# Idle transposes on TensorE in the first attention stage, with the first loads reordered

## The chip, the cores and the metric

The kernel runs on one core of one Trainium2 chip. A core has five engines that run their own instruction streams side by side [...]: TensorE (PE in the profile: matrix products, and transposes done as products with an identity), VectorE (DVE), ScalarE (ACT), GpSimd (POOL) and SyncE (SP, which here only issues DMA transfers). The metric is the device time of one execution in microseconds (us). Times of a kernel are given as the median of several executions, with the lowest and the highest. The profile is of one further execution, taken by the hardware profiler.

## The reference

The reference is attention with a threshold, followed by two dense layers with an ELU between them, all in float32:

```python
batch, n_heads, seq, head_dim = (8, 8, 576, 64)
scale = 1.0 / np.sqrt(q.shape[-1])
scores = scale * np.matmul(q, k.transpose(0, 1, 3, 2))
thresh = np.max(scores, axis=-1, keepdims=True) - tau
scores = np.where(scores >= thresh, scores, -1000000000.0)
scores = scores - np.max(scores, axis=-1, keepdims=True)
attn = np.exp(scores)
attn = attn / (np.sum(attn, axis=-1, keepdims=True) + 1e-09)
attn_out = np.matmul(attn, v)
# (B,H,S,D) -> (B*S, H*D): 4608 tokens of 512
h = x @ w_in                       # 512 x 2048
g = np.where(h > 0.0, h, alpha * (np.exp(np.minimum(h, 0.0)) - 1.0))
out = g @ w_out                    # 2048 x 512
```

`tau` is one number. The inputs of the dense layers' weights come as 64-bit floats and are converted to 32 bits on the chip, piece by piece.

## The kernel before

The kernel goes through 32 pairs of heads (8 sequences of 4 pairs). A pair has five steps: four with 128 queries of each of the two heads, and one with the last 64 queries of both. It is written in stages. The first stage is the first sequence, pairs 0 to 3, with only attention and some weight conversion in it; from the second stage on the dense layers' products are mixed in. In the first stage each head of a step passes through these parts, in the order that the framework's scheduler chooses (it orders by dependencies and its own estimates; the later stages stand under `manual_schedule`, where the order is the written one).

The start of the kernel: `tau` is read first and five small values are made of it, then the first pair's queries and keys are loaded and turned by VectorE, which puts the head dimension on the partitions:

```python
ident = wstage.tile([P, P], FP32, name="ident", bufs=1)
make_identity(nc, ident)

tau_sb = const.tile([P, 1], FP32, name="tau_sb")
nc.sync.dma_start(tau_sb, tau.to_broadcast([P, 1]))
pos = const.tile([P, 1], FP32, name="pos")
nc.vector.tensor_scalar(pos, tau_sb, 0.0, None, ALU.is_ge)
# ... keep, nkeep, far, ntau: five more small VectorE operations

def load(pr, parts=("qm", "km", "v"), shared=False):
    # ...
    for name, src in (("qm", q), ("km", k)):
        # ...
        for i in range(2):
            for d in range(2):
                r = (2 * i + d) * T
                nc.sync.dma_start(m[r : r + T],
                    src[b, 2 * j + i].rearrange("(j t) d -> t j d", t=T)[:, :, d * T : (d + 1) * T])
    # ... then four transfers of v into vm and vd

def prep_q(pr):   # VectorE turns the queries
    nc.vector.transpose(qT, raws[pr]["qm"].rearrange("p j d -> p (j d)"))
def prep_k(pr):   # and the keys
    nc.vector.transpose(kT[:, TAIL:], raws[pr]["km"].rearrange("p j d -> p (j d)"))

load(0)
prep(0)       # prep_q, copy_q, prep_k, copy_k
load(1)
```

The parts of one head in the first stage: scores on TensorE, maximum on VectorE, bias and bound on GpSimd, exponential on ScalarE, mask and sum on VectorE, division on GpSimd:

```python
def scores(pr, i, hs):
    # one of three PSUM buffers "sc"; two products of 288 keys for each head
    nc.tensor.matmul(scs[h][:, a, :HALF], qs[r], kT[r, k0 : k0 + HALF], start=True, stop=True)

def exponentials(pr, i, hs):
    nc.vector.tensor_reduce(st["mx"][:, cs], src[:, :, :, :HALF], axis=AX.XY, op=ALU.max)
    nc.gpsimd.tensor_scalar(st["nb"][:, cs], st["mx"][:, cs], nkeep, 1.0, ALU.mult, ALU.mult)
    nc.gpsimd.tensor_scalar(st["th"][:, cs], st["mx"][:, cs], 1.0, ntau, ALU.mult, ALU.add)
    nc.scalar.activation(e, st[h][:, :, :HALF], AF.Exp, bias=st["nb"][:, h : h + 1], scale=keep)

def masks(pr, i, hs):
    nc.vector.scalar_tensor_tensor(wv, sc[:, :, :HALF], st["th"][:, h : h + 1], e, ALU.is_ge, ALU.mult,
                                   accum_out=sm[:, h : h + 1])
    # ... 1 / (sum + 1e-9) into rs

def normalize(pr, i, hs):
    nc.gpsimd.tensor_scalar(wv, wv, st["rs"][:, h : h + 1], 1.0, ALU.mult, ALU.mult)
```

Then the weights `w` of a step are transposed on TensorE in groups of one to four 128x128 blocks. Each group has a PSUM buffer `rt` (two of them), and ScalarE copies it out to `wT`. A step of 128 queries has three groups (9 transposes), the step of the last queries has two (6):

```python
def transpose(dst, src):
    nc.tensor.matmul(dst, src, ident, is_transpose=True, skip_group_check=True)

def turn_parts(pr, i):
    # ...
    def room():
        return psum["t"].tile([P, NC, P], FP32, name="rt", tag="rt")

    def chunks(c0, c1):
        rt = room()
        for c in range(c0, c1):
            transpose(rt[:, c - c0], w[:, c * P : (c + 1) * P])
        return lambda: to(slice(g0, g0 + NT), slice(c0, c1), rt[:, : c1 - c0])   # ScalarE copies
    # ...
```

Last come the products with the values, `pv`, from `wT` (18 products for each half of a pair). The loop of the first stage:

```python
heads = [(pr, i, [h]) for pr, i in steps[:per_seq] for h in heads_of(i)]    # 36 heads
begin(*heads[0])                    # scores and exponentials
for n, (pr, i, hs) in enumerate(heads):
    if n + 1 < len(heads):
        begin(*heads[n + 1])
    # ... a piece of the dense layers' weights is loaded or converted now and then
    finish(pr, i, hs)               # masks and normalize
    if len(turned) > 1:
        behind(*turned.popleft())   # products with the values
    if n and hs == [0]:
        turn(*heads[n - 1][:2])     # transposes of the step before
        turned.append(heads[n - 1][:2])
```

## Time and profile before

| what | value |
|---|---|
| device time, median of 3 executions | 1376.99 us |
| lowest and highest | 1374.53 and 1379.93 us |
| span of the profiled execution | 1385.3 us |
| PE busy | 1338.2 us (97% of the span) |
| DVE busy | 1059.7 us (76%) |
| POOL busy | 834.4 us (60%) |
| ACT busy | 625.1 us (45%) |

Busy shares are averages over the whole span. The change touches the first stage alone, which in this profile takes about the first 112 us, so stretches of that part are what to read: the profile can give each engine's busy time for any stretch, and the timeline of an engine with the operation that it waited for. In such rows `sc` is the scores' product, `rt` a transpose, `pv` a product with the values; `x8` counts records, and a float32 matrix product of the scores or values leaves two records, a transpose one. Lines such as L238 are lines of the kernel's source. PEclk is the share of TensorE's full clock that was granted; it is shown as 1.00 where the trace holds no record of it, which is the case for the first 27.6 us.

### The profile page before, as it was taken

To read this page: it belongs to the slowest core of one execution; us is meant where nothing else is said; L and a number is where in the kernel's file an instruction comes from. 1 tells how busy PE (TensorE), PEld (TensorE's weight loads), DVE (VectorE), ACT (ScalarE), POOL (GpSimd) and SP (SyncE) were. 2 spreads that over 40 slices of the span, in tenths; PEclk is the share of its full clock that TensorE was granted. 3 is DMA by queue.
4 is the path that set the end of the run, shared out by engine and by line. 5 is a ranking of instruction groups with operands and counts; after the bars stand their busy time and mean duration, and the time that the engine had idled before them with its cause. 6 is when DMAs were issued, how large, how long until landed. Compare 5 with 4: busy or idle time off the path is not lost.

```text
span 1385.3 us, 21952 instructions
## 1 busy us (share of the span) xinstructions
PE 1338.2 (97%) x6566; PEld 993.5 (72%) x6566; DVE 1059.7 (76%) x2364; ACT 625.1 (45%) x1371; POOL 834.4 (60%) x1345
## 2 busy tenths in 40 slices
PE   7897889999999999999999999999999999999998
PEld 4554645746777777767777777777777777888886
DVE  6778885888879887869789878988888875545433
ACT  4666655225454554536363636354544453312320
POOL 4657774778657574747476756656575746425523
PEclk9999999999999999999999999999999999999999
DMA  5235552589798989898889989888889885321311
GB/s 114 58 72 143 142 143 62 165 239 263 221 253 222 273 221 241 225 256 235 225 234 249 251 225 256 225 239 216 250 234 263 232 243 172 123 69 55 102 57 31
DMA packets 316342, 259.82 MB, mean 188 GB/s; under 512 B 208320, under 2 KB 272320, under 8 KB 316224
## 3 DMA queue, kind: packets, MB, share of 16 engines
q1 hardware_dynamic: 316224, 258.42, 67.8%
q8 instruction: 53, 0.87, 0.3%
q14 instruction: 65, 0.53, 0.1%
HBM read 167.84 MB, written 90.51 MB: 186 GB/s over the span
## 4 chain that ended last, share of the span: by engine, by line
PE 79%; DVE 7%; POOL 4%; DMA 3%; ACT 3%; issue 2%; SPq 1%; DVEq 0%; POOLq 0%; ACTq 0%
PE f L1001 27%; PE f L846 25%; PE sc L238 12%; PE pv L388 8%; PE pv L384 2%; PE f L435 2%; PE f L475 2%; DMA there<-x 2%; DVE w L265 2%; PE rt L277 1%; ACT e L253 1%; POOL wtop L143 1%; POOL w L274 1%; DVE wtop L137 1%; DVE mx L248 1%
## 5 line engine op out<-in xcount | busy, mean ns | idle before, releaser
L274 POOL TENSOR_SCALAR w<-w,rs 128x576 f32<-128x576 f32 x288 | 246.1, 860 | 108.8 <-DVE rs L1111 75.2
L1085 DVE TENSOR_REDUCE mx<-sc 128x1 f32<-128x576 f32 x207 | 148.0, 752 | 88.5 <-PE sc L238 88.5
L238 PE MATMUL sc<-kT,qT 64*128 64x288 f32 x1024 | 185.5, 445 | 20.9 <-DVE w L265 11.5
L348 DVE STREAM_TRANSPOSE x<-w 128x512 f32<-128x512 f32 (+1 forms) x350 | 182.6, 569 | 8.2 <-POOL w L274 8.2
L1095 ACT ACTIVATE e<-sc,nb,keep 128x576 f32<-128x576 f32 x207 | 172.1, 831 | 7.0
L1104 DVE SCALAR_TENSOR_TENSOR w<-sc,th,e 128x576 f32<-128x576 f32 x207 | 163.4, 812 | 9.4 <-ACT e L1095 1.2
L1093 ACT ACTIVATE nb<-mx,nkeep 128x1 f32<-128x1 f32 x207 | 61.4, 297 | 233.0 <-DVE mx L1085 233.0
L238 PEld LDWEIGHTS sc<-kT,qT 64*128 64x128 f32 x1024 | 102.3, 193 | 86.5 <-issue 52.8
L846 PE MATMUL f<-xt,sw 128*128 128x256 f32 x512 | 128.8, 389 | 1.5 <-DMA sw<-win_sums 1.0
L846 PE MATMUL f<-xt,w_in_sb 128*128 128x256 f32 x512 | 124.5, 382 | 0.3 <-ACT w L860 0.2
L1089 POOL TENSOR_SCALAR th<-mx,ntau 128x1 f32<-128x1 f32 x207 | 54.4, 264 | 112.7 <-DVE mx L1085 112.5
L846 PEld LDWEIGHTS f<-xt,sw 128*128 128x128 f32 x512 | 93.3, 190 | 30.1 <-issue 14.6
L253 ACT ACTIVATE e<-sc,nb,keep 128x576 f32<-128x576 f32 x81 | 65.1, 830 | 104.7 <-POOL nb L249 103.9
L846 PEld LDWEIGHTS f<-xt,w_in_sb 128*128 128x128 f32 x512 | 96.1, 190 | 18.9 <-ACT xs L400 4.6
L1001 PE MATMUL f<-w_out_sb,s 128*128 128x256 f32 x448 | 109.4, 387 | 0.0
L1001 PE MATMUL f<-w_out_sb,g 128*128 128x256 f32 x448 | 107.4, 382 | 0.5 <-DVE g L901 0.5
L1001 PE MATMUL f<-t,s 128*128 128x256 f32 x448 | 106.6, 380 | 0.3 <-POOL s L938 0.3
L846 PE MATMUL f<-x,w_in_sb 128*128 128x256 f32 x448 | 105.8, 379 | 0.0
L1001 PEld LDWEIGHTS f<-w_out_sb,s 128*128 128x128 f32 x448 | 82.3, 190 | 23.0 <-issue 11.6
L1001 PEld LDWEIGHTS f<-w_out_sb,g 128*128 128x128 f32 x448 | 84.0, 190 | 16.6 <-issue 3.8
L865 POOL TENSOR_TENSOR u<-u,w 128x256 f32<-128x256 f32 x64 | 49.0, 766 | 77.3 <-ACT u L860 77.3
L1001 PEld LDWEIGHTS f<-t,s 128*128 128x128 f32 x448 | 84.1, 190 | 13.7 <-POOL s L938 2.7
(162 smaller groups left out, 2581.3 us busy)
## 6 DMA issues: line engine op xcount, KB each, us to landing
there<-x SPq DMA_DIRECT2D x500, 144.0 KB, 4.3
wTb<-there SPq DMA_DIRECT2D x75, 576.0 KB, 4.8
wTa<-there SPq DMA_DIRECT2D x50, 576.0 KB, 4.5
sw<-win_sums SPq DMA_DIRECT2D x62, 384.0 KB, 4.8
t<-wout_sums SPq DMA_DIRECT2D x45, 512.0 KB, 5.5
qm<-in_q_dram SPq DMA_DIRECT2D x128, 72.0 KB, 4.4
vm<-in_v_dram SPq DMA_DIRECT2D x64, 128.0 KB, 4.3
wst<-in_moe_w_in_dram SPq DMA_DIRECT2D x16, 512.0 KB, 4.6
```

The lines of the kernel that those rows point to most:

```text
L238: nc.tensor.matmul(scs[h][:, a, :HALF], qs[r], kT[r, k0 : k0 + HALF], start=True, stop=True)
L253: nc.scalar.activation(e, st[h][:, :, :HALF], AF.Exp, bias=st["nb"][:, h : h + 1], scale=keep)
L274: nc.gpsimd.tensor_scalar(wv, wv, st["rs"][:, h : h + 1], 1.0, ALU.mult, ALU.mult)
L348: nc.vector.transpose(x[:, :, c0 : c0 + nc_], src.rearrange("p (c g n) -> p g c n", c=nc_, n=T))
L388: nc.tensor.matmul(pv[h * D : (h + 1) * D, g0 * T : g1 * T], vm[:, h, c], wT[:, g0:g1, h * (NC + 1) + c], start=False, stop=(c == NC - 1), ...
L846: nc.tensor.matmul(loc["banks"][place], left[:, j], right[:, j], start=(begins and j == 0), stop=(j == 1), skip_group_check=True)
L1001: nc.tensor.matmul(place(m), lhs, rhs, start=(begins and v == 0), stop=(v == RU - 1), skip_group_check=True)
L1085: nc.vector.tensor_reduce(st["mx"][:, h : h + 1], st[h][:, :, :HALF], axis=AX.XY, op=ALU.max)
L1089: nc.gpsimd.tensor_scalar(st["th"][:, h : h + 1], st["mx"][:, h : h + 1], 1.0, ntau, ALU.mult, ALU.add)
L1093: nc.scalar.mul(st["nb"][:, h : h + 1], st["mx"][:, h : h + 1], nkeep)
L1095: nc.scalar.activation(e, st[h][:, :, :HALF], AF.Exp, bias=st["nb"][:, h : h + 1], scale=keep)
L1104: nc.vector.scalar_tensor_tensor(wv, sc[:, :, :HALF], st["th"][:, h : h + 1], e, ALU.is_ge, ALU.mult, accum_out=st["sm"][:, h : h + 1])
```

## The change

Three things change, all in the first stage.

1. Ahead of the first data, 28 transposes of the identity into an `rt` buffer are put on TensorE. Their results are never read. Each later group of transposes in the first stage gets four of the same ahead of it, into its own buffer, where the real ones then overwrite them. They are meant to keep TensorE active, and so its clock up, while it would otherwise wait.
2. The first pair's keys are loaded by ScalarE's DMA queue, beside the queries on SyncE's.
3. `tau` is read, and its small values made, after the first queries and keys have been asked for and turned; the values `v` of the first pair come after it. This opening now stands under `manual_schedule`.

```diff
-    tau_sb = const.tile([P, 1], FP32, name="tau_sb")
-    nc.sync.dma_start(tau_sb, tau.to_broadcast([P, 1]))
-    pos = const.tile([P, 1], FP32, name="pos")
-    nc.vector.tensor_scalar(pos, tau_sb, 0.0, None, ALU.is_ge)
     ... (the other small values)
+    def read_tau():
+        nc.sync.dma_start(tau_sb, tau.to_broadcast([P, 1]))
+        nc.vector.tensor_scalar(pos, tau_sb, 0.0, None, ALU.is_ge)
     ... (the other small values)
-    def load(pr, parts=("qm", "km", "v"), shared=False):
+    def load(pr, parts=("qm", "km", "v"), shared=False, queue=nc.sync):
     ...
-                    nc.sync.dma_start(
+                    queue.dma_start(
     ...
+    def idle(rt, n):
+        for _ in range(n):
+            transpose(rt[:, 0], ident)
+        return rt
     ...
         def room():
-            return psum["t"].tile([P, NC, P], FP32, name="rt", tag="rt")
+            return idle(psum["t"].tile([P, NC, P], FP32, name="rt", tag="rt"), 4 if "f" not in psum else 0)
     ...
-    load(0)
-    prep(0)
-    load(1)
+    with tc.manual_schedule():
+        load(0, ("qm",))
+        load(0, ("km",), queue=nc.scalar)
+        idle(psum["t"].tile([P, NC, P], FP32, name="rt", tag="rt"), 28)
+        prep_q(0)
+        prep_k(0)
+        copy_k(0)
+        copy_q(0)
+        read_tau()
+        load(0, ("v",))
+        load(1)
```

`"f" not in psum` holds in the first stage only. There are 54 groups of transposes in it, so 216 idle transposes beside the first 28.

## Prediction

> **What bounds the kernel now.** The page's chain that ended last is 79% PE, so I looked for where PE loses time. The change touches the first stage only, so I read that stage alone: first the timeline of PE, to see at what rate it works and where the stage ends, then busy time by stretch.

> ```profile
> 8.52 4.20 PE L238 MATMUL sc<-kT,qT 64*128 64x288 f32 x12 [8.52 <-DVE kT L200]
> 14.39 3.22 PE L238 MATMUL sc<-kT,qT 64*128 64x288 f32 x10 [1.68 <-DVE w L265]
> 17.54 1.97 PE L277 MATMUL rt<-ident,w 128*128 128x128 f32 x8
> ...
> 20.70 1.33 PE L277 MATMUL rt<-ident,w 128*128 128x128 f32 x5
> ...
> 28.05 0.60 PE L277 MATMUL rt<-ident,w 128*128 128x128 f32 x4
> 28.58 1.23 PE L238 MATMUL sc<-kT,qT 64*128 64x288 f32 x4
> ```

> Columns: start, duration, then the operation and, in brackets, the wait before it. At 17.54 eight transposes take 1.97 us and at 20.70 five take 1.33: three more cost 0.64, so 0.213 each. Later (102.71) eight take 1.04 us against 0.60 for four at 28.05: 0.11 each. So TensorE ran at half rate until about 28 us, although the clock column shows 1.00 there: no record exists before 27.6 us. The scores agree: four records take 2.26 us at 65.83 and 1.23 at 28.58. The stage ends with the last transposes, which the timeline puts at 110.97 plus 0.88, so about 111.6 once the modelled tail is taken off.

> ```profile
> 8.40:27.64 19.24, 17.45 (x53) 12.11 (x54) 12.76 (x36) 8.41 (x14) 8.35 (x24) 1.00 0.54 119
> 27.64:65.18 37.54, 33.92 (x183) 19.64 (x181) 30.41 (x84) 26.25 (x55) 25.18 (x51) 1.00 0.33 76
> 65.18:75.42 10.24, 9.59 (x25) 4.92 (x27) 6.38 (x21) 3.65 (x6) 5.31 (x12) 0.50 0.00 0
> 75.42:111.70 36.28, 34.36 (x191) 20.55 (x187) 26.38 (x73) 25.11 (x54) 22.72 (x42) 1.00 0.48 102
> ```

> Columns: stretch, length, busy time of PE, weight loads, DVE, ACT, POOL, then clock and DMA. PE is busy 95.3 of 103.3 us: 17.45 + 9.59 = 27.0 us in the two slow stretches, and 33.92 + 34.36 = 68.3 us in the two fast ones. In the fast stretches it lacks only 3.62 + 1.92 = 5.5 us. So this stage is PE's even at full clock, with DVE next (75.9 us busy). That fact decides what an extra transpose costs.

> The opening waits for the keys:

> ```profile
> 1.18 2.04 SPq L179 DMA_DIRECT2D qm<-in_q_dram  x4
> 3.27 2.12 SPq L179 DMA_DIRECT2D km<-in_k_dram  x4
> ...
> 5.42 0.78 DVE L195 STREAM_TRANSPOSE qT<-qm 128x576 f32<-128x576 f32 x1 [1.19 <-DMA qm<-in_q_dram]
> 7.68 0.78 DVE L200 STREAM_TRANSPOSE kT<-km 128x576 f32<-128x576 f32 x1 [1.49 <-DMA km<-in_k_dram]
> ```

> SyncE needs about 0.53 us for each issue, so the keys are asked for only after the queries, land at 7.66 and let PE start at 8.52.

> [...] PE is almost without a gap from 14.4 us on and stays slow until 27.6. Scores of the first stage use 64 of 128 rows, and the clock rises at 27.64, just after transposes and four full-height scores (`qd`). [...]

> [...] The trace before has no stretch of transposes alone. [...]

> [...] Before, issuing is indeed in series (2.04 + 2.12 us), while the DMA engines are already 75% busy from 4 to 8 us. So only part of 2.1 us can be won.

> **The change, part by part.**

> *Earlier keys and later `tau`.* Without `tau` first, SyncE starts at 0.74 instead of 1.18, and ScalarE issues the keys beside it, done by about 2.9. The last transfer before took 2.77 us from issue to landing; allowing for eight transfers sharing the engines, I put both landings near 6.0. Two turns of 0.78 give 7.5 instead of 8.5. The small `tau` operations (six of about 0.15 us) then stand behind the turns on DVE but beside the scores on PE. Gain: 1.0 us.

> *The first 28.* The identity is ready at about 1.4 us (its second GpSimd operation). 28 x 0.213 = 6.0 us at half rate, so they end at 7.5 at the latest, about when the keys are turned. [...] They cost nothing, or a few tenths.

> *Full clock throughout.* The slow 27.0 us of PE work become 13.5: gain 13.5 us at most. PE's work of the stage is then 13.5 + 68.3 = 81.8 us.

> *216 idle transposes.* 54 groups x 4 x 0.11 = 23.8 us more PE work. They come ahead of the real ones in PE's own order, so they are free only where PE would have waited anyway. All waits of the stage before are 103.3 - 95.3 = 8.0 us. The waits for POOL (the divided weights) can be filled; those for ACT (a free `rt` buffer) cannot, as the idle ones need the buffer too, nor those for DVE ahead of scores. I leave 2 us unfilled.

> *Sum.* Start 7.5, work 81.8 + 23.8 = 105.6, remaining waits 2.0: the stage ends at 115.1 instead of 111.6, +3.5 us. The changed order of the scheduler and the later stages, whose order is written and the same, I take as neutral. 1377.0 + 3.5 = 1380 us, rounded.

> So the chosen story is: the clock is mended as meant, but the stage is TensorE's own, and the idle work costs about what the clock brings.

> **Rivals.**

> *A. The idle work is really idle.* If a full clock made DVE and POOL the bound, PE would have gaps for all of it. For it: DVE is busy 75.9 us, and with 10 to 15 us of latency the stage could take 90 to 95 us; the groups were presumably put where PE waits. Against it: 81.8 + 23.8 leaves no such gaps. If half of the idle work hid, the stage would end 8 us earlier than in my sum: 1372 us.

> *B. Transposes do not hold the clock up.* Then the slow stretches stay, and 216 transposes cost up to 0.213 each: in a wholly slow stage 46 us. With slow stretches as before, the stage is longer by about 23.8 x 1.3 = 31 us less 6 of filled waits, near 1400 us. [...]

> *C. Only the opening counts.* The four-fold groups lie beside work, the clock comes up early at the start, but the later stretch at half clock is not seen in most executions of the kernel before (the times before spread over 5.4 us, about what that stretch costs: half of 9.6). Then less is gained from the clock than the profile says, and the idle work is paid in full: 1377 + 3.5 + 4.8, about 1385 us.

> *D. The end of the stage is hidden.* After 111.6 us PE waits until 116.3 for the next step's masks, so a little lateness of transposes could vanish; but the next step's scores (109.80) come in PE's order behind the idle ones, and their maximum on DVE follows at once. I expect no hiding.

> **Range and chances.** My sum is the difference of terms of 13.5 and 23.8 us, each good to perhaps 2, and a guess on filled waits good to 3. Rival A sets the low end, 1370; C and part of B the high end, 1388. 2% is 27.5 us: faster by that would need more than the whole clock gain and is nearly excluded (1%); slower by that needs B (3%, as B may also come in part). The rest, 96%, is within 2%.

> **What would show it.** In the profile after: the transposes at the start take 0.213 us each and then 0.11, with the clock up before 8 us (if not, B); scores start near 7.5 us (opening); no stretch at half clock in the first stage; idle `rt` rows of some 24 us; PE without waits of more than 2 to 4 us; last transposes of the stage at about 115 us. If that mark is at 108 or less, PE had room that I did not see, and A holds. If the mark is right and the total is not, the time lies in later stages, which I took as unchanged.

## The result, and the profile after

The changed kernel takes 1391.07 us (median of four executions, 1387.47 to 1395.79), the kernel before, run beside it on the same chip, 1375.85 us. The ratio is 1.0108, with a 95% interval of 1.0069 to 1.0146: the change makes the kernel about 15 us slower. The prediction was 1380 us with a range that ended at 1388. It had the right sign and far too small a size: +3.5 us where +15 were measured.

First the question of where. The first stage ends for TensorE (PE) some 4 us before the first mask of the second stage. That mask starts at 114.6 us in the profile of before and at 128.0 in that of after. From there to the end of the span it is 1270.8 us before and 1262.2 after. So the later stages did not lose anything; the profiled execution of before was itself long there (its span of 1385.3 us is far above what the median leaves room for). A second profile of the kernel before, taken later (`again_before`), has that mask at 111.3 and 1262.2 us from there to the end. Against it after has 16.7 us more in the first stage and nothing behind it. **The whole loss lies in the first stage.** I therefore compare that stage, and not spans.

Busy time of after by stretch of its first stage; columns are stretch, length, busy time and count of PE, weight loads, DVE, ACT, POOL, then PEclk, DMA share, GB/s:

```profile
8.00:70.20 62.20, 57.06 (x359) 39.48 (x359) 48.11 (x129) 36.33 (x71) 35.72 (x80) 1.00 0.41 87
70.20:73.61 3.41, 3.41 (x12) 1.94 (x13) 2.35 (x7) 2.09 (x4) 2.49 (x4) 0.50 0.00 0
73.61:100.92 27.31, 24.04 (x158) 16.51 (x155) 18.80 (x48) 15.59 (x32) 14.98 (x30) 1.00 0.47 98
100.92:107.75 6.83, 6.83 (x22) 3.39 (x22) 2.77 (x11) 1.68 (x3) 3.34 (x6) 0.50 0.00 0
107.75:125.20 17.45, 17.06 (x119) 12.00 (x115) 8.00 (x21) 8.26 (x18) 5.21 (x13) 1.00 0.33 88
```

Before had two half-clock stretches in the stage, to 27.64 us and from 65.18 to 75.42. After has two much shorter ones, 3.41 and 6.83 us, at other places. In both traces every record of a change of the clock lies a whole number of times 3.413 us from the first such record of its trace (in after 5.35, 70.20, 73.61, 100.92 and 107.75 us; in before 27.64, 65.18 and 75.42); a stretch of 3.41 us from one point of this grid to the next is called a window below. The clock was largely mended, though not wholly. But the stretches now reach to 125 us instead of 111.7. What fills them shows in PE's groups of this stretch (busy time, mean ns of one, then the idle time before them and what ended it):

```profile
L236 PE MATMUL sc<-kT,qT 64*128 64x288 f32 x136 | 35.2, 439 | 2.6 <-DVE pos L83 1.4 <-DVE w L263 1.2
L275 PE MATMUL rt<-ident 128*128 128x128 f32 x216 | 34.8, 286 | 3.7 <-ACT wTb L297 2.2 <-ACT wTa L297 1.5
L275 PE MATMUL rt<-ident,w 128*128 128x128 f32 x168 | 28.1, 278 | 3.9 <-POOL w L272 3.6
```

The 216 idle transposes are a group as heavy as the scores (35.2 us). The busy column carries the modelled tail of each, so it overstates them; counted from start to start (0.109 us each, and 0.213 for the eight at half clock) they take 24.4 us. And the line of the real transposes shows that a wait of 3.6 us for POOL's weights is still there. Now the opening, PE with the loads and the first turn:

```profile
0.73 2.13 ACTq L177 DMA_DIRECT2D km<-in_k_dram  x4
0.73 2.02 SPq L177 DMA_DIRECT2D qm<-in_q_dram  x4
1.46 5.15 PE L275 MATMUL rt<-ident 128*128 128x128 f32 x28 [1.46 <-POOL ident masks.py:199]
6.52 0.78 DVE L193 STREAM_TRANSPOSE qT<-qm 128x576 f32<-128x576 f32 x1 [6.52 <-DMA qm<-in_q_dram]
8.01 2.20 PE L236 MATMUL sc<-kT,qT 64*128 64x288 f32 x12 [1.40 <-DVE pos L83]
```

The 28 transposes start at 1.46 us. They end at 6.61 and not at 7.5, because they ran at half rate for only part of the time: they start 0.213 us apart up to 5.35 us and 0.109 apart from there. Twelve score records then take 2.20 us, where before the first twelve took 4.20: the clock is up when the first scores begin. That is the part of the change that did just what it was meant to.

**A budget of the stage.** The profile's busy column hides short gaps under modelled tails, so I counted the starts of PE's records instead. Each kind of record has a time of its own at full clock, read off runs of equal records (0.24 us for 288 columns, 0.109 us for a transpose). Inside a half-clock stretch, half of a record's own time there is counted as "half clock". Gaps of up to 0.2 us, nearly all between one kind of product and the next, are "short gaps"; longer ones are "waits". The stage ends here with the start of the last scores of the second stage's first step, which come just before its last transposes. All in us; each is good to about 1, and the rows add up to the end to 0.2.

| kernel | first score | real work, full clock | idle transposes, full clock | half clock | short gaps | waits | end of stage |
|---|---|---|---|---|---|---|---|
| before | 8.5 | 66.4 | 0 | 12.5 | 13.2 | 10.1 | 110.6 |
| after | 8.0 | 64.1 | 23.5 | 4.7 | 12.3 | 11.4 | 124.0 |
| after - before | -0.5 | -2.3 | +23.5 | -7.8 | -0.9 | +1.3 | +13.4 |
| prediction | -1.0 | 0 | +23.8 | -13.5 | 0 | -6.0 | +3.5 |

### The profile page after: what moved, and what is told of

It is laid out like the page before. It is cut to its first block, busy times and chain, and to the rows that moved or that the text cites. A ratio compares the mean times of both kernels' runs of the same rounds, so it can differ in the third digit from the quotient of the medians.

```text
span 1390.2 us, 22412 instructions
## 1 busy us (share of the span) xinstructions
PE 1352.2 (97%) x6810; PEld 1013.0 (73%) x6810; DVE 1062.4 (76%) x2364; ACT 625.0 (45%) x1371; POOL 834.9 (60%) x1345
## 4 chain that ended last, share of the span: by engine, by line
PE 80%; DVE 8%; POOL 5%; ACT 3%; issue 2%; DMA 1%; DVEq 0%; SPq 0%; POOLq 0%; ACTq 0%
PE f L1013 27%; PE f L858 27%; PE sc L236 11%; PE pv L392 8%; PE pv L388 2%; ACT e L251 2%; DVE w L263 2%; PE f L439 2%; PE f L479 2%; PE rt L275 1%; POOL w L272 1%; DVE mx L246 1%; DVE wtop L135 1%; POOL wtop L141 1%; DVE wtop L134 1%
## 5 line engine op out<-in xcount | busy, mean ns | idle before, releaser
L236 PE MATMUL sc<-kT,qT 64*128 64x288 f32 x1024 | 174.8, 432 | 12.6 <-DVE w L263 11.2
L236 PEld LDWEIGHTS sc<-kT,qT 64*128 64x128 f32 x1024 | 95.6, 187 | 76.0 <-issue 54.3
L858 PEld LDWEIGHTS f<-xt,sw 128*128 128x128 f32 x512 | 93.3, 190 | 29.0 <-issue 13.5
L877 POOL TENSOR_TENSOR u<-u,w 128x256 f32<-128x256 f32 x64 | 49.0, 765 | 76.7 <-ACT u L872 75.9
## 6 DMA issues: line engine op xcount, KB each, us to landing
vm<-in_v_dram SPq DMA_DIRECT2D x64, 128.0 KB, 4.3
```

Of the source, the lines that this page charges most:

```text
L858: nc.tensor.matmul(loc["banks"][place], left[:, j], right[:, j], start=(begins and j == 0), stop=(j == 1), skip_group_check=True)
```

## The theories

**Theory 1: the idle work is paid in full.** The transposes do not stand where PE waits. They are put ahead of real transposes in PE's own order, and PE reaches them when the weights are ready and there is work to do. The waits fall elsewhere and stay. Then the time must grow with the count of idle transposes by nearly 0.109 us each.

**Theory 2: the other order costs.** With new instructions and `manual_schedule` the scheduler orders the stage otherwise, and the real work, its gaps or waits became dearer.

**Theory 3: the opening costs.** The later `tau`, the loads on two queues or the 28 transposes delay the first heads.

The trace of after speaks for theory 1 already. This is its timeline around one head; all engines, with some rows left out:

```profile
72.25 1.46 POOL L272 TENSOR_SCALAR w<-w,rs 128x576 f32<-128x576 f32 x2
...
76.59 0.66 PE L275 MATMUL rt<-ident 128*128 128x128 f32 x4
...
77.09 0.60 PE L275 MATMUL rt<-ident,w 128*128 128x128 f32 x4
```

POOL has divided the weights by 73.71 us. PE comes to the group at 76.59, almost 3 us later, because it was busy with other products. There it first does four idle transposes, then the four real ones at 77.09; four more idle ones at 77.52 and real ones at 77.96 follow. Each block puts off the next real work by 0.44 to 0.50 us. There are 54 such groups. In 46 the weights were ready before the idle block had run, and 22.0 of the 25.9 us that the blocks take (with the short gaps beside them) stand ahead of weights that were ready. Only 3.9 us lie where PE would have waited.

And where PE does wait long, the idle ones had been used up earlier, because they need only the free buffer. PE alone, a little earlier in the same trace:

```profile
65.82 0.60 PE L275 MATMUL rt<-ident 128*128 128x128 f32 x4
66.35 0.75 PE L236 MATMUL sc<-kT,qT 64*128 64x288 f32 x2
68.89 0.66 PE L275 MATMUL rt<-ident,w 128*128 128x128 f32 x4 [1.79 <-POOL w L272]
```

The block for the group of 68.89 ran at 65.82, three us too early, and PE then stood still for 1.79 us. The clock fell at 70.20, 1.31 us after this wait. The other fall looks the same: a block ran at 97.51, and PE waited for its weights until 100.57, 0.35 us before the clock fell at 100.92:

```profile
100.57 0.83 PE L275 MATMUL rt<-ident,w 128*128 128x128 f32 x4 [1.79 <-POOL w L272]
```

## The experiments

Each edit is against the changed kernel, unless it says otherwise. Times are medians; ratios are to the kernel before, run on the same chip, with their 95% interval.

### Without the groups (`e_open`)

```diff
-            return idle(psum["t"].tile(...), 4 if "f" not in psum else 0)
+            return idle(psum["t"].tile(...), 0 if "f" not in psum else 0)
```

> The opening alone: 28 idle transposes, keys on the second queue, tau later; no idle transposes ahead of the groups. Before is 1376 us, after the change 1391. Theory 1 (idle work ahead of the groups is paid in full and fills no wait): without it only the gains are left, the clock is up from about 5 us on and the scores start at 8.0, so 1368 to 1373, and the first stage ends 5 to 9 us earlier than the 111.6 us of before. Theory 2 (the loss comes from the other order that the scheduler chose, which here is almost that of before): also 1368 to 1373. Theory 3 (the opening itself costs, through the first transfers or through ScalarE's table load that it pushes back): 1380 or more.

Measured: 1377.59 us, ratio 1.0009 (0.9988 to 1.0030). Taking the 216 away brings nearly all of the loss back: 13.5 us. That is theory 1's cost, less the half-clock time and the better order (below) that went with the groups. But the gain that I expected of the opening is missing. The busy time by stretch, columns as above, shows why:

```profile
4.79:15.04 10.25, 6.21 (x36) 4.49 (x34) 7.44 (x23) 2.38 (x3) 2.80 (x10) 1.00 0.73 122
15.04:25.27 10.23, 10.15 (x32) 6.92 (x32) 7.33 (x21) 5.80 (x11) 6.18 (x18) 0.50 0.52 131
```

The clock is up at 4.79 us, but PE is busy for only 6.21 of the next 10.25 us, as it waits for data and for the first masks, and the clock falls again at 15.04, for 10 us. So the early full clock bought little here: the ratio is 1.0009. The second slow stretch of before is there again, from 62.82 to 73.06.

### One, and eight, for each group (`e_one`, `e_eight`)

```diff
-            return idle(psum["t"].tile(...), 4 if "f" not in psum else 0)
+            return idle(psum["t"].tile(...), 1 if "f" not in psum else 0)   # e_one; 8 in e_eight
```

> The change with 1 idle transpose ahead of each group instead of 4. Theory 1: 54 x 0.11 = 5.9 us above the opening alone, 1374 to 1379, and 17 to 18 us below the change. Theory 2: the order is close to that of before, so it should be within 3 us of the opening alone. Theory 3: within 6 us of the change, near 1386.

> The change with 8 idle transposes ahead of each group instead of 4. Theory 1: 216 x 0.11 = 23.8 us more than the change, 1411 to 1418, since nothing is left to fill. Theory 2: the order of the real work is already a changed one, so the loss should not double: 1385 to 1400. Theory 3: 1391 plus what the idle work costs, 1400 to 1418, which does not tell it from theory 1; the other two runs do.

Measured: 1382.67 us for one (1.0058, 1.0006 to 1.0111) and 1411.58 us for eight (1.0262, 1.0238 to 1.0286). From four to eight the time grows by 20.5 us; 216 more at 0.109 make 23.5, beside which the stage has about 2 us less real work and 1.5 less half clock. Eight leave only 6.8 us of the stage at half clock, two windows, and still each further one is paid. With eight, the blocks in front of ready weights are 52 of 54. PE's timeline of `e_eight`:

```profile
125.87 1.09 PE L275 MATMUL rt<-ident 128*128 128x128 f32 x8
126.80 0.60 PE L275 MATMUL rt<-ident,w 128*128 128x128 f32 x4
127.24 1.04 PE L275 MATMUL rt<-ident 128*128 128x128 f32 x8
128.11 0.60 PE L275 MATMUL rt<-ident,w 128*128 128x128 f32 x4
```

No bracket stands behind any of them: nothing is waited for, and eight of every twelve transposes make results that nobody reads. With one per group the clock is not held: 34 us of the stage are at half clock. (Its profiled execution was long, 11 us above its median, and the interval of its ratio is wide; it bears on the sign, not on the size.)

### The groups without the opening (`e_groups`)

This one is the kernel before with the groups alone.

```diff
+    def idle(rt, n):
+        for _ in range(n):
+            transpose(rt[:, 0], ident)
+        return rt
-            return psum["t"].tile([P, NC, P], FP32, name="rt", tag="rt")
+            return idle(psum["t"].tile(...), 4 if "f" not in psum else 0)
```

> The kernel before with 4 idle transposes ahead of each group and nothing else of the change. Theory 1: the opening's gain of 5 to 8 us is missing, so 1395 to 1400. Theory 2: like the change, 1390 to 1397. Theory 3: the opening was the loss, so 1375 to 1382.

Measured: 1405.17 us, ratio 1.0206 (1.0180 to 1.0233), 14 us more than the change, and above what I expected, as I had not counted the clock. So the opening is worth something in company: without it the stage has 13.9 us of half-clock loss instead of 4.7, and the idle transposes that fall into slow stretches cost double (in after, 0.213 us each instead of 0.109). For theory 3 it is the wrong way round: with the opening taken out, the time rises.

### The loads alone (`e_load`)

```diff
-        idle(psum["t"].tile([P, NC, P], FP32, name="rt", tag="rt"), 28)
-            return idle(psum["t"].tile(...), 4 if "f" not in psum else 0)
+            return idle(psum["t"].tile(...), 0 if "f" not in psum else 0)
```

> The opening without its 28 idle transposes: keys on the second queue and tau later, no idle work at all. The opening alone was 1377.6 us against 1374.9 of before. If the first 28 raise a clock that is worth something, this run has half clock to about 27 us as before has, and ends its first stage 1 to 3 us later than the opening alone, 1377 to 1381 us. If the 28 are worth nothing because the clock is lost again at 15 us, it is within 1 us of the opening alone and of before, 1374 to 1378. The scores should start near 8.0 us in either case.

Measured: 1372.74 us, ratio 0.9974 (0.9965 to 0.9982, from 20 executions). No idle transpose at all, keys on ScalarE's queue and `tau` later: this version beats both kernels, if only by 0.26%. After its start at half rate (the first twelve score records take 4.14 us) it has one slow stretch in the stage, this row of its busy time by stretch, and from 29.20 to the end of the stage none in this execution:

```profile
15.55:29.20 13.65, 13.65 (x41) 8.82 (x40) 9.90 (x31) 6.54 (x12) 7.57 (x20) 0.50 0.37 97
```

Theory 3 falls for the loads and for `tau`. For the 28 transposes it does not fall as clearly: without the groups they come out some 4 us dearer than the loads alone (see the repeats below).

### Idle work at the start only (`e_early`)

The thought: keep the clock up past the first heads (PE is busy for 6.21 of 10.25 us of them in `e_open`), and then stop paying.

```diff
+    counts = [10, 10, 4, 4, 4, 4]
-            return idle(psum["t"].tile(...), 4 if "f" not in psum else 0)
+            return idle(psum["t"].tile(...), counts.pop(0) if counts else 0)
```

> The opening, and idle transposes ahead of the first six groups only: 10, 10, 4, 4, 4, 4. The first twenty fall in the wait between the third and the fourth head's scores. If the opening gains nothing because PE then stands still for the first masks and the clock falls (half clock from 15 to 25 us in the opening alone), these hold it up, 5 us of slow work go, 1 to 2 us of idle work are paid: 1372 to 1375, the first stage ends 2 to 4 us before that of the opening alone. If idle work is paid in full wherever it stands, 36 x 0.11 = 4 us come on top: 1379 to 1382.

Measured: 1384.41 us, ratio 1.0051 (1.0031 to 1.0071). A miss. With the 36 transposes the clock stayed up from 7.05 to 37.77 us, and they cost only 3.9 us. But slow stretches came later instead, from 37.77 to 48.01 and from 65.08 to 75.32: half-clock loss is 9.05 us, as without them (9.15 in `e_open`). Why they came is not shown. The stage ends at 111.3, 3 us after that of `e_open`, in an execution 4 us shorter than the median.

### A third buffer for the weights (`e_open_w3`, `e_after_w3`)

If PE's waits came from DVE having no free buffer for the weights, a third one would remove them. Once on the opening alone, once on the whole change.

```diff
-            st["w"] = wpool[0].tile([P, 2 * S], FP32, name="w")
+            st["w"] = wpool[0].tile([P, 2 * S], FP32, name="w", **({"bufs": 3} if wpool[0] is wstage else {}))
```

> The opening alone with a third buffer for the weights w, so that masks need not wait for the transposes of two steps earlier (4 to 6 us of such waits of VectorE in the first stage). If PE's own waits of 10 to 12 us come round through that buffer, they fall to 6 to 8 us and the time to 1371 to 1375. If they come from elsewhere (scores' buffers, copies by ScalarE), nothing changes: 1376 to 1379.

> The change with the same third buffer. The idle work is paid in full whatever the buffers: 12 to 17 us above the opening with the third buffer, so 1385 to 1391. If instead the two buffers are what keeps idle work from hiding, the distance shrinks to under 8 us: 1376 to 1383.

Measured: 1386.28 us on the opening alone (1.0065, 1.0048 to 1.0082) and 1387.77 us on the change (1.0089, 1.0068 to 1.0110). On the opening alone DVE's wait for a free weight buffer went from 7.3 us to 0, and came back as DVE's wait for scores (8.6 to 21.2 us); PE's waits stayed at 12.1 and 11.5 us. So this buffer was not what makes PE wait. The time missed both of my figures: it is 8.7 us above `e_open`. In its profile the stage has 34 us at half clock after the opening (14.29 to 27.95, 41.60 to 48.43 and 89.39 to 103.04 us), against 20.5 in `e_open`; why the third buffer does this is not shown.

But `e_after_w3` settles another question. No record of half clock lies in its first stage (whether thanks to the third buffer or to where the windows lay, I can't tell):

```profile
8.10:120.30 112.20, 103.44 (x662) 71.07 (x662) 80.09 (x215) 64.04 (x126) 62.08 (x130) 1.00 0.39 86
```

Here the change reached its aim completely, and the stage still ends at 119.3 us, 8.7 later than before (11.9 later than `again_before`). By the same budget its idle work takes 23.5 us and its real work 64.2, with waits of 11.5: with all the clock's loss gone, only the idle work is large enough to explain the later end. This is the clearest single piece of evidence for theory 1. The distance to `e_open_w3`, though, is 1.5 us and not the 12 to 17 that I expected, and less than the 8 that I had put down to hiding. The stages show why it is not hiding: `e_open_w3` ends its stage at 115.5 us, 3.9 earlier, with 15.5 us of half-clock loss where `e_after_w3` has none. There the clock that the idle work saves nearly pays for it.

### The small differences again (`again_before`, `again_load`, `again_open`, `open_22`)

Loads alone looked 5 us better than loads plus 28 transposes. To see whether this holds, the same kernels were run again, and one with 22 instead of 28, which leaves the order of PE's other work exactly that of before. `again_before` is the kernel before, `again_load` is `e_load`, `again_open` is `e_open`.

```diff
-        idle(psum["t"].tile([P, NC, P], FP32, name="rt", tag="rt"), 28)
+        idle(psum["t"].tile([P, NC, P], FP32, name="rt", tag="rt"), 22)      # open_22, on e_open
```

> The kernel before once more, for a second trace of its first stage. If the stretch at half clock near 65 to 75 us comes from a thin place in this order of work, it recurs within a few us of there. [...] Time 1374 to 1379 us either way.

> The opening without idle transposes once more. It was 1372.7 us and had no stretch at half clock between 30 and 110 us. If its order of work has no thin place, that is so again and the time is 1371 to 1375. If it was the lie of the windows, a stretch of 7 to 10 us appears and the profiled time is 3 to 5 us longer.

> The opening with its 28 idle transposes once more; 1377.6 us before, half clock from 15 to 25 and from 63 to 73 us. Thin place in the order: the second stretch recurs, 1375 to 1379. Lie of the windows: it may not, and then the profiled execution is near 1371.

> The opening with 22 idle transposes, with which the scheduler leaves TensorE exactly the order of before. If idle work at the start is good for 3 us (heads up to the ninth came 2.8 us earlier with the 28) and the order of the later work decides the rest, it is 2 to 4 us under before: 1371 to 1374. If the early gain is always given back, it equals before: 1374 to 1378.

| kernel | time | ratio | 95% interval |
|---|---|---|---|
| `again_before` | 1377.57 | 1.0008 | 0.9999 to 1.0017 |
| `again_load` | 1374.22 | 0.9986 | 0.9974 to 0.9999 |
| `again_open` | 1378.19 | 1.0022 | 1.0005 to 1.0039 |
| `open_22` | 1378.37 | 1.0012 | 0.9999 to 1.0024 |

The order holds: loads alone are faster than before both times, and the 28 added to them, with the other order that they bring, take about 4 us back (4.85 and 3.97). `open_22` has PE's order of before and a first mask at 11.5 us instead of 13.3, and yet it is no faster than before: the early gain is given back. Where it goes can be seen in the slow stretch that returns, almost at the same time, in `again_open` (63.00 to 73.24 us), `again_before` (62.24 to 72.48) and `open_22`, whose row is:

```profile
65.11:75.35 10.24, 10.24 (x29) 4.81 (x29) 5.35 (x18) 3.15 (x5) 5.04 (x12) 0.50 0.00 0
```

It is in all five profiles of kernels with before's order or the opening's (these three, before and `e_open`), and in neither of the two with the order of the loads alone, which differs from before's in a few places. So with that order the clock fell there each time (at 62.24 to 65.18 us), whether the stage began early or late; what in the order does it is not shown. But the second profile of the loads alone is not free of a slow stretch. It has one at another place:

```profile
88.20:95.03 6.83, 6.83 (x20) 3.48 (x21) 5.00 (x17) 3.11 (x5) 4.02 (x12) 0.50 0.01 2
```

That execution took 1378.18 us, the longest of its twelve. This is what I had expected if the lie of the windows decides, and not the order alone; the two are not told apart. Whether the stretch missing near 62 us accounts for the 4 us stays open too: the second stage's first mask is at 110.4 and 112.6 in the two profiles of the loads alone, and at 112.2 in both of the opening, a difference smaller than that between two profiles of one kernel. The 4 us rest on the times alone. So of theory 3 one part stands: without the groups, the 28, or the order that comes with them, cost something.

## Why the prediction was wrong

**The sign and the reason were right.** "The stage is TensorE's own, and the idle work costs about what the clock brings": the first half holds in every run with idle work ahead of the groups (all are slower than before). Where it failed is in two terms of the sum.

**Failed step 1: "I leave 2 us unfilled".** I let the idle transposes fill 6.0 of 8.0 us of waits. On balance they filled none: waits, counted by starts, are 10.1 us before and 11.4 after, an error of 7.3 us, the largest of all. Two things were wrong. The waits are not where the idle work is. PE's waits in the first stage of before, from its list of waits (total, times, longest; in us), were there to read:

```profile
PE sc L238 <- DVE w L265: 2.4, 3, 1.7
PE rt L277 <- ACT wTb L293: 2.0, 3, 1.2
PE pv L384 <- ACT wTa L293: 1.0, 1, 1.0
PE rt L277 <- POOL w L274: 0.9, 2, 0.6
PE sc L238 <- DVE rs L268: 0.7, 1, 0.7
PE pv L384 <- ACT wTb L293: 0.7, 1, 0.7
```

By my own rule only those for POOL could be filled: 0.9 us. I wrote the rule down and then did not apply it to this list. And filled time comes back: the idle work delays what follows, and PE then waits for other things (3.9 us of the blocks lay in waits, and yet the waits grew by 1.3). The top of the list of after:

```profile
PE rt L275 <- POOL w L272: 3.6, 2, 1.8
PE rt L275 <- ACT wTb L297: 2.2, 6, 0.8
PE rt L275 <- ACT wTa L297: 1.5, 4, 0.5
```

The waits for POOL grew, though these are the ones that idle transposes were to fill, because each block runs as soon as its buffer is free. In every variant of the study PE's waits are 9 to 13 us.

**Failed step 2: "Full clock throughout".** Of 13.5 us I expected all back; 7.8 came (against `again_before`, whose half-clock loss is 8.35 us, 3.7). After keeps 10.24 us of half clock in two stretches; in the 3.41 us before each of them PE's busy time is 1.62 us. This is an error of 5.7 us. It is also a mis-sized term to start with: half-clock loss of the kernel before is not a constant, 12.5 us in one profile and 8.35 in the other.

**What offset them.** The order that I took as neutral was not, and it helped. Real work at full clock fell from 66.4 to 64.1 us. Scores of 64 rows that begin less than 0.15 us after the one before them number 23 at full clock after 28 us, against 9 before: the scheduler put those of two heads side by side more often. So theory 2 has the wrong sign. With the start 0.5 us less good than predicted, the idle work 0.3 cheaper and short gaps 0.9 less, the errors are 0.5 - 0.3 + 5.7 + 7.3 - 2.3 - 0.9 = 10.0, and 3.5 + 10.0 is the 13.4 us measured, to rounding.

**Right, step by step.** The idle transposes cost 23.5 us (said: 23.8). The clock is up (at 5.35 us) before the first scores. The scores start at 8.0 (said: 7.5; the queries landed later than my 6.0, for `qT` is turned at 6.52, and the keys are turned after them). The later stages are neutral (1262.2 us in both).

**The rivals.** A, that the idle work really hides, is refuted by `e_eight` and `e_after_w3`. (Its 1372 us was summed wrongly: half of 23.8 is 11.9, of which my sum hid 6.0 already, so the stage would end 5.9 us earlier and not 8.) B, that transposes do not hold the clock up, is refuted by the opening: this row of after covers a stretch in which PE does nothing else,

```profile
1.93:5.35 3.42, 3.42 (x18) 3.42 (x17) 0.00 (x0) 1.28 (x1) 0.00 (x0) 1.00 1.37 167
```

and the first clock record, at 5.35 us, is at full clock. (The 1.00 of the row is no record: in it the transposes start 0.213 us apart, from 5.35 us on 0.109.) C came nearest by its number, 1385 us, and that the idle work is paid in full is what the runs show. But its premise fails: the second slow stretch of before is not seldom seen, it is in both profiles of that kernel. D, that the end of the stage is hidden, is refuted by the marks: the 16.7 us by which after is later than `again_before` at the first mask of the second stage are 16.7 at the end of the span.

**What stays open.** Why PE's waits stay at 9 to 13 us whatever is done: a third weight buffer does not change it, and more buffers for scores or transposes were not tried. And why the two profiles of the loads alone lack the slow stretch near 62 us, and one of them has another at 88.

## What to carry to other kernels

Idle work that is meant for an engine's waits must be put where that engine waits, and instructions placed ahead of real work in the engine's own order were mostly not there (22.0 of the 25.9 us of the blocks stood ahead of weights that were ready): before adding it, list that engine's waits in the stage, see which of them the new work could run in, and charge all the rest in full. When the clock falls, read the stretch before the fall (here a wait of 1.79 us stood shortly before each of two): starting earlier did not remove the slow stretch near 62 us, and filling everywhere cost 23.5 us to win 7.8 of clock. Compare such a change by a mark at the end of the stage, since spans of single executions of one kernel differed by nearly 12 us here (1385.3 and 1373.6 for the kernel before).
